# Casting weight loads, a woven first out-projection and pinned engine order in a fused attention and feed-forward kernel

## The chip, the cores and the metric

The kernel runs on one core of a Trainium2 chip. The metric is the device time of one execution in microseconds (us). Each version was run four times beside the kernel before (four to seven runs) on the same chip. All runs here lie within 1.5% of the fastest of the same kernel.

Engines: PE is TensorE's matmul, PEld its weight load, DVE is VectorE, ACT is ScalarE, POOL is GpSimd, SP is SyncE (it issues DMAs).

## The reference, cut to what matters

```python
# q, k, v: (8, 8, 576, 64) float32; w_in: (512, 2048); w_out: (2048, 512)
scores = scale * np.matmul(q, k.transpose(0, 1, 3, 2))
mask = (rel >= 0) & (rel < 64)                    # rel: query minus key position; causal window of 64
attn = softmax(np.where(mask, scores, -1e9))
x = np.matmul(attn, v).transpose(0, 2, 1, 3).reshape(4608, 512)
h = np.maximum(x @ w_in, 0.0)
out = (h * h @ w_out).astype(np.float32)
```

The 4,608 tokens are 36 chunks of 128, or 9 groups of 512. The kernel does the matmuls in 16 bits. Per chunk there is an attention (transposes of k and q, scores, values, transpose of x); per group an up-projection, a squared relu and an out-projection.

## The kernel before

Five names are used all through: T (transposes of k and q), S (scores, exp and mask), V (values, division by the row sums), X (transpose of x) and U (up-projection of one chunk, in four quarters). A scheduler that the framework runs may reorder each engine's instructions, unless the engine is pinned to the emitted order; the kernel before pins none.

```python
    def load_w_in():                       # float32 through a ring of four buffers
        def one(quar, c):
            ws = wst.tile([P, FQ], FP32, name="ws", tag="ws")
            nc.sync.dma_start(out=ws[:], in_=moe_w_in[c * P:(c + 1) * P, quar * FQ:(quar + 1) * FQ])
            nc.vector.tensor_scalar(out=w_in_sb[:, c, quar * FQ:(quar + 1) * FQ], in0=ws[:],
                                    scalar1=W_SCALE, scalar2=None, op0=ALU.mult)
        # ... 16 of them; w_out likewise, cast on GpSimd

    def transposes(i):                     # T: 8 transposes on PE, then
        # ... halo of the last chunk's keys copied on VectorE
        nc.vector.tensor_copy(out=kT[:, :, 64:192], in_=ps[:, 0])
        nc.scalar.activation(out=qT[:], in_=ps[:, 1], func=AF.Copy, scale=1.0)

    def values(i):                         # V
        for half in range(2):
            # ... 8 matmuls into av
            nc.vector.reciprocal(out=rden[:], in_=av[:, :, 64:65])
            nc.vector.tensor_tensor(out=x_sb[:, 4 * half:4 * half + 4, :], in0=av[:, :, 0:D],
                                    in1=rden[:].to_broadcast([P, 4, D]), op=ALU.mult)

    # after an up-projection's matmuls into hps: relu on ScalarE, square on VectorE
            nc.scalar.activation(out=hrelu[:], in_=hps[:], func=AF.Relu)
            nc.vector.scalar_tensor_tensor(out=..., in0=hps[:], scalar=0.0, in1=hrelu[:],
                                           op0=ALU.max, op1=ALU.mult)

    # ---- order of emission
    load(0)
    for s in load_w_in(): s()
    NFIRST = 8                             # eight chunks one by one, before any out-projection
    for i in range(1, NV - 1): load(i)
    # ... attention of chunk 0 with warm-up matmuls between
    for i in range(1, NFIRST):
        up = ffn_up_chunk(i)
        up[0](), V(i + 1), T(i + 2), up[1](), up[2](), X(i + 1), S_(i + 2), up[3]()
    for g in range(1, NTB + 1):            # steady part: three streams, evenly interleaved
        streams = [(ffn_out(g - 1), 0.0, 1.0)]
        if g >= 2 and g < NTB: streams.append((ffn_up(g), 0.0, 1.0))
        if g + 1 < NTB: streams.append((attention(g + 1), 0.0, 0.95))
        # ...
```

The softmax here doesn't subtract the row's maximum and nothing guards it: scores larger than these inputs give would overflow.

Of the kernel before, what the change touches and what calls it, by code (L numbers as in the profile page):

```python
# [13 lines left out]


def weave(*streams):

    keyed = []
    for s, (steps, lo, hi) in enumerate(streams):
        n = len(steps)  # L20
        for i, step in enumerate(steps):
            keyed.append((lo + (hi - lo) * (i + 0.5) / n, s, i, step))
    keyed.sort(key=lambda e: e[:3])
    return [e[3] for e in keyed]
# [3 lines left out]
def kernel(  # L28
# [17 lines left out]
    W_SCALE = 100.0  # L46
    OUT_SCALE = 1.0 / (W_SCALE * W_SCALE)
# [6 lines left out]
    wst = ctx.enter_context(tc.tile_pool(name="wst", bufs=4))  # L54
    stage = ctx.enter_context(tc.tile_pool(name="stage", bufs=15))
    st16 = ctx.enter_context(tc.tile_pool(name="st16", bufs=8))
    attw = ctx.enter_context(tc.tile_pool(name="attw", bufs=3))
# [8 lines left out]

    ident = const.tile([P, P], FP16, name="ident")
    make_identity(nc, ident[:])





    base = const.tile([P, 64], FP16, name="base")
    nc.gpsimd.memset(base[:], BIG)
    nc.gpsimd.affine_select(
        out=base[:], in_=base[:], compare_op=ALU.is_ge, fill=0.0, base=-1,
        pattern=[[-1, 64]], channel_multiplier=1,
    )
    nc.gpsimd.affine_select(  # L80
        out=base[:], in_=base[:], compare_op=ALU.is_ge, fill=0.0, base=64,
        pattern=[[1, 64]], channel_multiplier=-1,
    )
# [10 lines left out]
    mask_first = make_mask("mask_first", 0)  # L94
    mask_inner = make_mask("mask_inner", None)
    mask_second = make_mask("mask_second", 1)

    w_in_sb = const.tile([P, DMC, DFF], FP16, name="w_in_sb")
    w_out_sb = const.tile([P, FFC, DM], FP16, name="w_out_sb")

    NV = 8
    v_evs = [const.tile([P, H, 66], FP16, name=f"v_ev{i}") for i in range(NV)]
    v_ods = [const.tile([P, H, 66], FP16, name=f"v_od{i}") for i in range(NV)]
    for i in range(NV):
        nc.vector.memset(v_evs[i][:, :, 64:65], 1.0)
        nc.vector.memset(v_ods[i][:, :, 64:65], 1.0)
    nc.vector.memset(v_ods[0][0:64, :, 0:D], 0.0)

    def load_w_in():
        steps = []  # L110
        FQ = DFF // 4

        def one(quar, c):
            ws = wst.tile([P, FQ], FP32, name="ws", tag="ws")
            nc.sync.dma_start(out=ws[:], in_=moe_w_in[c * P:(c + 1) * P,  # L115
                                                      quar * FQ:(quar + 1) * FQ])
            nc.vector.tensor_scalar(  # L117
                out=w_in_sb[:, c, quar * FQ:(quar + 1) * FQ], in0=ws[:],
                scalar1=W_SCALE, scalar2=None, op0=ALU.mult)

        for quar in range(4):
            for c in range(DMC):
                steps.append(lambda quar=quar, c=c: one(quar, c))
        return steps

    def load_w_out():
        def one(f):
            ws = wst.tile([P, DM], FP32, name="ws2", tag="ws")
            nc.sync.dma_start(out=ws[:], in_=moe_w_out[f * P:(f + 1) * P, :])
            nc.gpsimd.tensor_copy(out=w_out_sb[:, f, :], in_=ws[:])  # L130

        return [lambda f=f: one(f) for f in range(FFC)]


    xTs = {}

    def xT_of(g):
        if g not in xTs:
            xTs[g] = xtp.tile([P, DMC, 512], FP16, name="xT", tag="xT")
        return xTs[g]  # L140

    q16s, k16s, qTs, kTs, pms, xs = {}, {}, {}, {}, {}, {}

    def load(i):

        sts = []
        for (src, nm) in ((k, "k"), (q, "q"), (v, "v")):
            st = stage.tile([P, H, D], FP32, name=f"{nm}_st", tag="st")
            b0, j0 = divmod(2 * i, NB)
            if j0 + 1 < NB:  # L150
                nc.sync.dma_start(  # L151
                    out=st[:], in_=src[b0, :, 64 * j0:64 * j0 + P, :].rearrange("h p d -> p h d"))
            else:
                nc.sync.dma_start(
                    out=st[0:64], in_=src[b0, :, 64 * j0:S, :].rearrange("h p d -> p h d"))
                nc.sync.dma_start(
                    out=st[64:P], in_=src[b0 + 1, :, 0:64, :].rearrange("h p d -> p h d"))
            sts.append(st)
        k16s[i] = st16.tile([P, H * D], FP16, name="k16", tag="k16")
        nc.gpsimd.tensor_copy(out=k16s[i][:], in_=sts[0][:].rearrange("p h d -> p (h d)"))  # L160
        q16s[i] = st16.tile([P, H * D], FP16, name="q16", tag="q16")
        nc.gpsimd.tensor_copy(out=q16s[i][:], in_=sts[1][:].rearrange("p h d -> p (h d)"))
        v_ev, v_od, v_next = v_evs[i % NV], v_ods[i % NV], v_ods[(i + 1) % NV]
        nc.gpsimd.tensor_copy(out=v_ev[:, :, 0:D], in_=sts[2][:])
        nc.gpsimd.tensor_copy(out=v_od[64:P, :, 0:D], in_=v_ev[0:64, :, 0:D])
        if i + 1 < NCK:
            nc.gpsimd.tensor_copy(out=v_next[0:64, :, 0:D], in_=v_ev[64:P, :, 0:D])

    def transposes(i):
        ps = ps_att.tile([P, 2, HP, P], FP16, name="qkT_ps", tag="ps_a")  # L170
        for s, src in enumerate((k16s, q16s)):
            for hp in range(HP):
                nc.tensor.transpose(out=ps[:, s, hp, :], in_=src[i][:, hp * P:(hp + 1) * P],  # L173
                                    identity=ident[:])
        kT = attw.tile([P, HP, 192], FP16, name="kT", tag="kT")
        if i > 0:
            nc.vector.tensor_copy(out=kT[:, :, 0:64], in_=kTs[i - 1][:, :, P:192])
        else:
            nc.vector.memset(kT[:, :, 0:64], 0.0)
        nc.vector.tensor_copy(out=kT[:, :, 64:192], in_=ps[:, 0])  # L180
        qT = attw.tile([P, HP, P], FP16, name="qT", tag="qT")
        nc.scalar.activation(out=qT[:], in_=ps[:, 1], func=AF.Copy, scale=1.0)  # L182
        kTs[i], qTs[i] = kT, qT

    def scores(i):
        sc = [ps_att.tile([P, HP, 2, 64], FP32, name=f"sc{hh}", tag="ps_a") for hh in range(2)]
        for hp in range(HP):
            for blk in range(2):
                for hh in range(2):
                    r0 = 64 * hh  # L190
                    nc.tensor.matmul(  # L191
                        sc[hh][:, hp, blk, :], kTs[i][r0:r0 + 64, hp, 64 * blk:64 * blk + P],
                        qTs[i][r0:r0 + 64, hp, 64 * blk:64 * blk + 64], start=True, stop=True)
        j0 = 2 * i % NB
        mask = mask_first if j0 == 0 else mask_second if j0 + 1 == NB else mask_inner
        pms[i] = []
        for hh in range(2):
            pm = attw.tile([P, HP, 2, 64], FP16, name=f"pm{hh}", tag=f"pm{hh}")
            nc.scalar.activation(out=pm[:], in_=sc[hh][:], func=AF.Exp,
                                 scale=1.0 / float(D) ** 0.5)  # L200
            nc.vector.tensor_tensor(out=pm[:], in0=pm[:], in1=mask, op=ALU.min)
            pms[i].append(pm)

    def values(i):
        x_sb = attw.tile([P, H, D], FP16, name="x_sb", tag="x_sb")
        for half in range(2):
            av = ps_att.tile([P, 4, 66], FP32, name="av", tag="ps_a")
            for h in range(4 * half, 4 * half + 4):
# [8 lines left out]
                out=x_sb[:, 4 * half:4 * half + 4, :], in0=av[:, :, 0:D],  # L217
                in1=rden[:].to_broadcast([P, 4, D]), op=ALU.mult)
        xs[i] = x_sb

    def to_xT(i):
        xt = ps_att.tile([P, DMC, P], FP16, name="xt_ps", tag="ps_a")
        for c in range(DMC):
            nc.tensor.transpose(out=xt[:, c, :], in_=xs[i][:, 2 * c:2 * c + 2, :],  # L224
                                identity=ident[:])
        nc.vector.tensor_copy(out=xT_of(i // 4)[:, :, (i % 4) * P:(i % 4 + 1) * P], in_=xt[:])  # L226

    def attention(g):

        steps = []  # L230
        fns = (transposes, scores, values, to_xT)
        for t in range(4 + len(fns) - 1):
            for s, fn in enumerate(fns):
                if 0 <= t - s < 4:
                    steps.append(lambda fn=fn, i=4 * g + t - s: fn(i))
        return steps

    def loads(g):
        return [lambda i=i: load(i) for i in range(4 * g, 4 * g + 4)]

# [3 lines left out]
    def ffn_up(g):  # L244
        h2s[g] = h2pool.tile([P, FFC, 512], FP16, name="h2", tag="h2")

        def one(f):
# [59 lines left out]




    load(0)
    for s in load_w_in():
        s()
# [55 lines left out]
```

## Time and profile before

| Kernel before | |
|---|---|
| time | 347.75 us median (347.43 to 350.61) |
| span of the profiled run | 345.9 us, mean granted TensorE clock 0.987 |
| first up-projection matmul, first out-projection matmul | 19.4 us, 71.4 us |
| first matmul of a full-group up-projection | 99.1 us |
| from there to the last matmul | 242.2 us |

The last three rows are starts of matmuls read from the trace. "The head" below is everything before the first matmul of a full-group (512-token) up-projection, "the steady part" what follows it.

Busy time of each engine by stretch of the kernel before (start:length, then busy us and count of instructions of each engine, granted clock, DMA share, GB/s):

```profile
40.00:50.00 10.00, 8.49 (x164) 7.49 (x162) 8.56 (x19) 5.66 (x11) 9.44 (x17) 1.00 0.99 256
50.00:60.00 10.00, 9.13 (x175) 8.14 (x173) 8.72 (x24) 6.45 (x12) 6.14 (x10) 1.00 0.76 245
60.00:70.00 10.00, 9.26 (x177) 8.22 (x175) 8.95 (x23) 5.70 (x11) 5.07 (x9) 1.00 0.82 209
...
92.00:330.00 238.00, 237.83 (x2038) 118.66 (x2036) 149.46 (x348) 122.27 (x217) 65.52 (x106) 1.00 0.40 101
```

In the chunked stage VectorE (third pair) is nearly as full as PE (first pair); from 92 to 330 us PE is idle for 0.17 us in 238.

### The profile page before, as it was taken

What the parts mean: (1) busy time and instruction counts of PE and PEld (TensorE: products, weight loads), DVE (VectorE), ACT (ScalarE), POOL (GpSimd) and SP (SyncE); (2) the same over time, 40 slices, a digit from 0 to 9 for tenths busy, and PEclk for the clock granted to TensorE, in tenths of its full rate; (3) what the DMA queues carried; (4) which work ended last, traced back from release to release, by engine and by line L of the source; (5) the groups of instructions that cost most, each with busy time, mean ns of one, the idle gap of its engine ahead of it and who ended that gap; (6) DMA issues with size and microseconds to landing.
All of it is one profiled execution on the core that took longest, in us unless ns stands there. A gap on an engine that the chain in (4) does not pass through costs nothing.

```text
span 345.9 us, 7917 instructions
## 1 busy us (share of the span) xinstructions
PE 324.3 (94%) x3146; PEld 178.2 (52%) x3146; DVE 207.9 (60%) x506; ACT 163.8 (47%) x289; POOL 121.5 (35%) x204
## 2 busy tenths in 40 slices
PE   1957888999999999999999999999999999999995
PEld 0346787875555555445545554455445544544442
DVE  2656988852666776676776657665675566544400
ACT  1123457544535646643664466436544654444411
POOL 4009895497753333316566544530000000000000
PEclk9996999999999999999999999999999999999998
DMA  7799987899972455546877757730011000000021
GB/s 200 249 252 239 234 247 252 207 230 228 243 172 61 93 121 123 121 124 155 212 185 182 170 135 184 185 87 27 23 45 36 30 32 32 30 30 32 35 88 62
DMA packets 122341, 46.65 MB, mean 135 GB/s; under 512 B 113600, under 2 KB 113600, under 8 KB 122304
## 3 DMA queue, kind: packets, MB, share of 16 engines
q1 hardware_dynamic: 122304, 46.15, 51.7%
q8 instruction: 24, 0.39, 0.5%
q14 instruction: 13, 0.11, 0.1%
HBM read 36.70 MB, written 9.44 MB: 133 GB/s over the span
## 4 chain that ended last, share of the span: by engine, by line
PE 83%; DVE 7%; DMA 5%; ACT 2%; SPq 1%; issue 1%; ACTq 0%
PE ops L296 37%; PE hps L250 28%; DMA ws<-in_moe_w_in_dram 5%; PE qkT_ps L173 4%; PE av L211 4%; PE xt_ps L224 2%; DVE h_397 L276 1%; DVE h_1087 L276 1%; DVE xT L226 1%; DVE w_in_sb L117 1%; PE hps_639 L271 1%; SPq L151 1%; SPq L115 0%; PE hps_1088 L271 0%; PE hps_1537 L271 0%
## 5 line engine op out<-in xcount | busy, mean ns | idle before, releaser
L250 PE MATMUL hps<-xT,w_in_sb 128*128 128x512 f16 x448 | 115.2, 379 | 0.0
L254 ACT ACTIVATE hrelu<-hps 128x512 f32<-128x512 f32 x112 | 66.8, 598 | 91.6 <-PE hps L250 90.9
L250 PEld LDWEIGHTS <-w_in_sb 128*128 128x128 f16 x448 | 43.7, 98 | 52.6 <-issue 0.3
L271 PEld LDWEIGHTS <-w_in_sb 128*128 128x128 f16 x512 | 31.2, 99 | 8.2 <-issue 3.9
L301 ACT ACTIVATE osb<-ops 128x512 f32<-128x512 f32 x36 | 21.6, 600 | 29.1 <-PE ops L296 28.9
L182 ACT ACTIVATE qT<-qkT_ps 128x512 f16<-128x512 f16 x36 | 21.5, 596 | 22.6 <-DVE kT L180 22.3
L216 DVE TENSOR_TENSOR x_sb<-av,rden 128x256 f16<-128x256 f32 x72 | 27.5, 415 | 0.1
L180 DVE COPY kT<-qkT_ps 128x512 f16<-128x512 f16 x36 | 15.2, 421 | 18.0 <-PE qkT_ps L173 17.8
L226 DVE COPY xT<-xt_ps 128x512 f16<-128x512 f16 x36 | 15.1, 420 | 12.7 <-PE xt_ps L224 12.7
L215 DVE RECIPROCAL rden<-av 128x4 f32<-128x4 f32 x72 | 11.4, 178 | 17.1 <-PE av L211 17.1
L255 DVE SCALAR_TENSOR_TENSOR h_5222<-hps,hrelu 128x512 f16<-128x512 f32 x16 | 11.1, 691 | 16.6 <-ACT hrelu L254 16.6
L296 PE MATMUL ops<-w_out_sb,h_1087 128*128 128x512 f16 x64 | 17.5, 380 | 0.0
L191 PEld LDWEIGHTS <-kT 64*128 64x128 f16 x576 | 11.0, 95 | 12.2 <-issue 9.6
L296 PE MATMUL ops<-w_out_sb,h_3120 128*128 128x512 f16 x64 | 16.5, 380 | 0.0
L296 PE MATMUL ops<-w_out_sb,h_2579 128*128 128x512 f16 x64 | 16.5, 380 | 0.0
L296 PE MATMUL ops<-w_out_sb,h_4199 128*128 128x512 f16 x64 | 16.5, 380 | 0.0
L296 PE MATMUL ops<-w_out_sb,h_3658 128*128 128x512 f16 x64 | 16.5, 380 | 0.0
L296 PE MATMUL ops<-w_out_sb,h_2041 128*128 128x512 f16 x64 | 16.5, 380 | 0.0
L296 PE MATMUL ops<-w_out_sb,h_4736 128*128 128x512 f16 x64 | 16.4, 379 | 0.0
L296 PE MATMUL ops<-w_out_sb,h_397 128*128 128x512 f16 x64 | 15.3, 380 | 0.0
L224 PE MATMUL xt_ps<-ident,x_sb 128*128 128x128 f16 x144 | 15.1, 222 | 0.1
L255 DVE SCALAR_TENSOR_TENSOR h_4736<-hps,hrelu 128x512 f16<-128x512 f32 x16 | 11.0, 689 | 6.8 <-ACT hrelu L254 6.4
(837 smaller groups left out, 611.1 us busy)
## 6 DMA issues: line engine op xcount, KB each, us to landing
out_dram<-osb SPq DMA_DIRECT2D x36, 256.0 KB, 2.2
k_st<-in_k_dram SPq DMA_DIRECT2D x32, 256.0 KB, 3.9
q_st<-in_q_dram SPq DMA_DIRECT2D x32, 256.0 KB, 4.0
v_st<-in_v_dram SPq DMA_DIRECT2D x32, 256.0 KB, 4.1
ws<-in_moe_w_in_dram SPq DMA_DIRECT2D x16, 256.0 KB, 4.2
k_st<-in_k_dram SPq DMA_DIRECT2D x8, 128.0 KB, 3.2
q_st<-in_q_dram SPq DMA_DIRECT2D x8, 128.0 KB, 3.0
v_st<-in_v_dram SPq DMA_DIRECT2D x8, 128.0 KB, 3.2
```

What stands on the lines that cost most here:

```text
L173: nc.tensor.transpose(out=ps[:, s, hp, :], in_=src[i][:, hp * P:(hp + 1) * P], identity=ident[:])
L180: nc.vector.tensor_copy(out=kT[:, :, 64:192], in_=ps[:, 0])
L182: nc.scalar.activation(out=qT[:], in_=ps[:, 1], func=AF.Copy, scale=1.0)
L216: nc.vector.tensor_tensor(out=x_sb[:, 4 * half:4 * half + 4, :], in0=av[:, :, 0:D], in1=rden[:].to_broadcast([P, 4, D]), op=ALU.mult)
L224: nc.tensor.transpose(out=xt[:, c, :], in_=xs[i][:, 2 * c:2 * c + 2, :], identity=ident[:])
L226: nc.vector.tensor_copy(out=xT_of(i // 4)[:, :, (i % 4) * P:(i % 4 + 1) * P], in_=xt[:])
L250: nc.tensor.matmul(hps[:], w_in_sb[:, c, f * P:(f + 1) * P], xT_of(g)[:, c, :], start=(c == 0), stop=(c == DMC - 1))
L254: nc.scalar.activation(out=hrelu[:], in_=hps[:], func=AF.Relu)
L255: nc.vector.scalar_tensor_tensor(out=h2s[g][:, f, :], in0=hps[:], scalar=0.0, in1=hrelu[:], op0=ALU.max, op1=ALU.mult)
L271: nc.tensor.matmul(hps[:, f, :], w_in_sb[:, c, (4 * fq + f) * P:(4 * fq + f + 1) * P], xT_of(g)[:, c, t0:t0 + P], start=(c == 0), stop=(c ...
L296: nc.tensor.matmul(hold["ps"][:], h2s[g][:, f, ts * P:(ts + 1) * P], w_out_sb[:, f, :], start=(f == 0), stop=(f == FFC - 1))
L301: nc.scalar.activation(out=osb[:], in_=hold["ps"][:], func=AF.Copy, scale=OUT_SCALE)
```

## The change

The intent: get both weights into 16 bits without VectorE, fill the wait for w_in with attention, give the VectorE-heavy chunk-by-chunk stage less to do, and fix the order of all engines to the emitted one. The core of the diff:

```diff
-        def one(quar, c):
-            ws = wst.tile([P, FQ], FP32, name="ws", tag="ws")
-            nc.sync.dma_start(out=ws[:], in_=moe_w_in[...])
-            nc.vector.tensor_scalar(out=w_in_sb[...], in0=ws[:], scalar1=W_SCALE, ...)
+    def load_w_in(quar):                    # casts from float32 on the way; w_out likewise
+        nc.gpsimd.dma_start(out=w_in_q[quar][:], in_=moe_w_in[...])
 ...
-        if i > 0:                           # halo copy of every chunk
-            nc.vector.tensor_copy(out=kT[:, :, 0:64], in_=kTs[i - 1][:, :, P:192])
+        if i % 4 == 0:                      # one boundary tile per group of four chunks
+            nc.vector.tensor_copy(out=kBs["b", g][:, :, 64:P], in_=kTs["k", g][:, :, 0:64])
 ...
+    def square(out, hps, hrelu):
+        nc.scalar.activation(out=hrelu, in_=hps, func=AF.Relu, scale=H_SCALE)
+        nc.vector.scalar_tensor_tensor(
+            out=out, in0=hps, scalar=0.0, in1=hrelu, op0=ALU.max, op1=ALU.mult)
 ...
+    E = mybir.EngineType
+    ctx.enter_context(tc.manual_schedule(engines={E.PE, E.Activation, E.DVE, E.Pool, E.SP}))
 ... loads of chunks 0 to 3, attention of 0 and part of 1 and 2, w_in behind the key casts of chunks 3 and 4, w_out behind that of chunk 5
+    V(1), S(2), X(1), warm(1), T(3), V(2), S(3), U(0, 0), X(2), U(1, 0), U(2, 0), V(3)
+    load_chunk(6)
+    U(0, 1), U(1, 1), X(3), U(2, 1), U(0, 2), U(1, 2), U(2, 2), U(3, 0), U(3, 1), T(4)
+    load_chunk(7)
+    U(3, 2), U(0, 3), S(4), U(1, 3), U(2, 3), U(3, 3), V(4), T(5), X(4), S(5)
 ... first out-projection, woven with attention of chunks 6 to 11 and U of 6 and 7
+    for i in range(6, 12):
+        t = 0.17 + 0.115 * (i - 6)
+        steps += [(t, T, i), (t + 0.06, S, i), (t + 0.15, V, i), (t + 0.21, X, i)]
 ... steady part, per group (positions are shares of the group)
+        steps = [((n + 0.5) / 16, out_proj, g - 1, n // 4, n % 4) for n in range(16)]
+            steps += [((f + 0.8) / 16, up, g, f) for f in range(FFC)]
+                i, t = 4 * G + j, 0.18 * j
+                    steps += [(t, T, i), (t + 0.07, S, i)]
+                steps.append((t + 0.17, V, i))
+                    steps.append((t + 0.25, X, i))
```

## The prediction

> **What bounds the kernel now.** TensorE. The table of stretches shows it busy 10.0 of every 10 us from 70 us to its last matmul at 341.8 us; only the head has slack. By the timeline the chunked up-projections (chunks 0 to 7) end at 75.4 us. I estimate: 75.4 to 341.8 us, less 1,024 matmuls of 512 columns at 0.216 us (four start 0.864 us apart), leaves 45 us for 28 chunks' attention, 1.6 us each. A chunk's up-projection, 64 matmuls, takes 3.7 us (16 in 0.92). Eight chunks at 5.3 us are 42.6 us: the head wastes 33 us.
>
> Where: first matmul at 4.4 us, a mask wait of 2.7 us, 26 warm-up matmuls in the trace; from 20 to 31 us waits for w_in (the chain has 5% w_in DMA; VectorE waits 12.1 us for it), with the granted clock at 0.5 to 0.6 from 26 to 30 us; then seven chunks at 6.4 us each. There VectorE is nearly full (8.6 to 9.0 of 10 us, 40 to 70 us). Its work per chunk, from the groups: key copies 0.33 + 0.42, masks 2 x 0.7, reciprocals 2 x 0.18, x 2 x 0.415, xT 0.42, four squarings at 0.69: 6.5 us.
>
> **What the change does.**
> 1. w_in comes as four 1 MB casting loads issued on GpSimd after chunks 0 to 3: no four-buffer ring, no 16 VectorE scalings (7.0 us). [...] No cast load is in the trace; plain w_in loads reached 352 to 379 GB/s for 2 us, about 250 in the mean. Attention of four chunks fills the time before w_in.
> 2. One pair of halo copies per group, not one copy per chunk.
> 3. The VectorE-bound head shrinks from eight chunks to six; the rest of group 1 and attention 8 to 11 run beside the first out-projection: PE has 31 us of work there, VectorE 26.
> 4. Order pinned; the steady part has the same arithmetic, so the same time at best.
>
> **Sum.** Chunks 0 to 3 land by 15 us (0.79 MB each at 250 GB/s), w_in, interleaved with chunks 4 and 5, by 32 to 36 us. After it: four quarter up-projections and chunks 4 and 5, 17 us with their chains. Head ends near 51 us (46 to 59). Then 1,024 x 0.216 + 7.4 + 30 x 1.6 = 277 us, 2 us of new waits, the 3.5 us tail, 1.8 us between span and measured time: 335 us. Without waits and with fast casts 327; slow casts give 343.
>
> **What would show it.** w_in's last quarter landing at 32 to 36 us; the first out-projection beginning near 51 us, not 71; no VectorE waits for w_in; PE about 10 of 10 from 52 us on; second out-projection to the end within 1% of before; the same tail.
>
> **What would make it wrong.** Casting loads well below 250 GB/s, or starved by chunk loads [...]: w_in at 45 us, or w_out late, and the gain halves. GpSimd issuing them late, behind casts that wait for DMA. Chunks 6 to 11 are needed every 3.8 us against 3.1 us of load: a late one stops the pinned PE. Pinned ACT and VectorE queues blocking in the steady part (1% is 2.7 us). The clock dropping around 17 to 25 us.
>
> Faster (under 340.8 us) 0.80, within 2% 0.17, slower 0.03. Prediction 335 us, 327 to 343.

## More of the kernel before

The profile page of before: busy times, two rows of the table of forty equal slices (digits are tenths busy), the chain that ended last, and three groups (name, shape, count | busy, mean ns | idle time just before, and what ended most of it).

```profile
PE 324.3 (94%) x3146; PEld 178.2 (52%) x3146; DVE 207.9 (60%) x506; ACT 163.8 (47%) x289; POOL 121.5 (35%) x204
PE   1957888999999999999999999999999999999995
DVE  2656988852666776676776657665675566544400
...
PE 83%; DVE 7%; DMA 5%; ACT 2%; SPq 1%; issue 1%; ACTq 0%
...
L182 ACT ACTIVATE qT<-qkT_ps 128x512 f16<-128x512 f16 x36 | 21.5, 596 | 22.6 <-DVE kT L180 22.3
L216 DVE TENSOR_TENSOR x_sb<-av,rden 128x256 f16<-128x256 f32 x72 | 27.5, 415 | 0.1
L215 DVE RECIPROCAL rden<-av 128x4 f32<-128x4 f32 x72 | 11.4, 178 | 17.1 <-PE av L211 17.1
```

PE is full after the head. The last line shows a healthy order on VectorE: the reciprocals wait for PE's values (17.1 us in all), that is, VectorE stands ready when they arrive.

## The result and the profile after

The changed kernel took 352.4 us median (351.49 to 352.79, four runs), against 347.75 us. Ratios here and below are the mean time of one kernel's runs over that of the other's of the same rounds, so not quite the ratio of the medians quoted; this one is 1.0111, with a 95% interval of 1.0071 to 1.015. It is 1% slower (the interval excludes 1), where 3.7% faster was predicted.

| | before | after | difference |
|---|---|---|---|
| first out-projection | 71.4 | 60.4 | -11.0 |
| first full-group up-projection (end of the head) | 99.1 | 97.1 | -2.0 |
| from there to the last matmul | 242.2 | 249.3 | +7.1 |
| span | 345.9 | 350.6 | +4.7 |

The first out-projection did start 11 us earlier, but it now carries work which before had been done ahead of it, so the milestone itself is no gain. At the end of the head 2 us were left of it, no more than single profiled runs scatter (see the table of milestones below), and the steady part gave back 7.

The profile page after, the same parts (the squarings had been split into many small groups on the page before):

```profile
PE 325.4 (93%) x3139; PEld 182.0 (52%) x3139; DVE 201.7 (58%) x475; ACT 164.8 (47%) x294; POOL 116.4 (33%) x191
PE   7749878889899999999999999999999999999995
DVE  3646756487757646764676467646764566433300
...
PE 73%; DVE 13%; ACT 5%; DMA 3%; SPq 2%; issue 2%; POOL 1%; ACTq 0%
...
L250 DVE SCALAR_TENSOR_TENSOR h<-hps,hrelu 128x512 f16<-128x512 f32 x144 | 99.2, 690 | 112.0 <-ACT hrelu L249 111.6
L168 ACT ACTIVATE qT<-qkT_ps 128x512 f16<-128x512 f16 x36 | 21.5, 597 | 61.1 <-DVE kT L167 61.1
```

PE's share of the chain fell from 83% to 73%, VectorE's rose from 7% to 13%, although VectorE has 6 us less work. ScalarE's query copies wait 61 us behind VectorE's key copies, 22 before. The stretches after:

```profile
40.00:50.00 10.00, 7.05 (x133) 6.02 (x131) 6.91 (x16) 5.90 (x11) 3.65 (x6) 0.97 1.20 191
50.00:60.00 10.00, 8.45 (x129) 7.85 (x127) 5.76 (x13) 3.90 (x8) 5.16 (x9) 0.86 1.15 217
60.00:70.00 10.00, 9.12 (x111) 5.32 (x109) 4.45 (x12) 3.94 (x8) 7.92 (x14) 1.00 1.03 208
70.00:80.00 10.00, 8.70 (x152) 6.47 (x150) 7.45 (x17) 5.21 (x11) 6.83 (x11) 1.00 0.96 208
...
92.00:330.00 238.00, 234.81 (x1974) 118.53 (x1975) 143.55 (x322) 117.92 (x212) 61.94 (x99) 1.00 0.45 99
```

No compute engine is full from 40 to 80 us: PE idles for 6.7 us in 40, and VectorE is less busy than before. The DMA engines are busy throughout (shares of 0.96 to 1.20), but of the loads PE's list of waits, of which the four longest follow, names only one of w_in, 3.4 us before the first up-projection. Even from 92 to 330 us PE idles for 3.2 us, where it had been 0.17. PE's longest waits in the changed kernel, and two of VectorE's (us in total, times, longest):

```profile
PE sc L193 <- ACT qT L168: 3.8, 10, 0.7
PE xt_ps L232 <- DVE x_sb L222: 3.6, 8, 1.0
PE hps L268 <- DMA w_in<-in_moe_w_in_dram: 3.4, 1, 3.4
PE av L217 <- DVE pm L206: 2.2, 6, 0.5
...
```

```profile
DVE h L250 <- ACT hrelu L249: 111.6, 124, 4.1
...
DVE rden L221 <- PE av L217: 0.2, 1, 0.2
```

The second fence is the symptom: VectorE waits for ScalarE's relu 124 times, and the reciprocals practically never wait for PE's values (0.2 us; 17.1 before). Nearly whenever values arrive, VectorE comes late to them. A piece of the trace of the changed kernel shows why (start us, duration, engine, line, operation, what it waited for):

```profile
45.08 0.60 ACT L249 ACTIVATE hrelu<-hps 128x512 f32<-128x512 f32 x1 [0.71 <-PE hps L268]
...
45.23 0.19 PE L217 MATMUL av<-v_ev,pm 128*64 128x65 f16 x1
...
45.71 0.69 DVE L250 SCALAR_TENSOR_TENSOR h<-hps,hrelu 128x512 f16<-128x512 f32 x1 [0.62 <-ACT hrelu L249]
46.32 0.17 DVE L221 RECIPROCAL rden<-av 128x4 f32<-128x4 f32 x1
46.53 0.42 DVE L222 TENSOR_TENSOR x_sb<-av,rden 128x256 f16<-128x256 f32 x1
...
47.01 0.28 PE L232 MATMUL xt_ps<-ident,x_sb 128*128 128x128 f16 x2 [1.03 <-DVE x_sb L222]
...
47.41 0.41 DVE L167 COPY kT<-qkT_ps 128x512 f16<-128x512 f16 x1
...
47.86 0.60 ACT L168 ACTIVATE qT<-qkT_ps 128x512 f16<-128x512 f16 x1 [2.18 <-DVE kT L167]
...
48.51 0.41 PE L193 MATMUL sc<-qT,kT 64*128 64x64 f16 x16 [0.67 <-ACT qT L168]
```

The values are there by 45.4 us. VectorE is idle, but its next instruction is a squaring, which needs a relu that ScalarE finishes only at 45.7. The squaring takes 0.69 us, then reciprocals and copies follow; PE has to wait 1.03 us for x and 0.67 us for the query copy. VectorE and ScalarE keep to the program's order in this trace: compared by line with the built program, all 475 instructions of VectorE and 293 of ScalarE's 294 (the other is a table load) start in the order in which it has them. So here a waiting instruction holds up ready ones behind it: the reciprocal at 46.32 comes 0.9 us after the last values. Whether the loss comes from it is for the experiments to say.

### The profile page after: what moved, and what is told of

Its sections match the earlier page's. It is cut to its first block, busy times and chain, and to the rows that moved or that the text cites. A ratio compares the mean times of both kernels' runs of the same rounds, so it can differ in the third digit from the quotient of the medians.

```text
span 350.6 us, 7832 instructions
## 1 busy us (share of the span) xinstructions
PE 325.4 (93%) x3139; PEld 182.0 (52%) x3139; DVE 201.7 (58%) x475; ACT 164.8 (47%) x294; POOL 116.4 (33%) x191
## 4 chain that ended last, share of the span: by engine, by line
PE 73%; DVE 13%; ACT 5%; DMA 3%; SPq 2%; issue 2%; POOL 1%; ACTq 0%
PE ops L285 31%; PE hps L256 26%; PE hps L268 6%; DVE h L250 5%; DVE pm L206 3%; ACT hrelu L249 3%; PE av L217 3%; PE qkT_ps L163 3%; PE sc L193 2%; SPq L81 2%; DVE x_sb L222 2%; DMA w_in<-in_moe_w_in_dram 2%; PE xt_ps L232 2%; DMA st<-in_v_dram 1%; ACT qT L168 1%
## 5 line engine op out<-in xcount | busy, mean ns | idle before, releaser
L250 DVE SCALAR_TENSOR_TENSOR h<-hps,hrelu 128x512 f16<-128x512 f32 x144 | 99.2, 690 | 112.0 <-ACT hrelu L249 111.6
L285 PE MATMUL ops<-w_out,h 128*128 128x512 f16 x576 | 145.6, 380 | 0.5 <-DVE h L250 0.5
L249 ACT ACTIVATE hrelu<-hps 128x512 f32<-128x512 f32 x144 | 85.9, 597 | 88.9 <-PE hps L256 69.1
L256 PE MATMUL hps<-xT,w_in 128*128 128x512 f16 x448 | 115.1, 379 | 0.0
L285 PEld LDWEIGHTS <-h 128*128 128x128 f16 x576 | 52.6, 98 | 57.2 <-issue 0.8
L256 PEld LDWEIGHTS <-w_in 128*128 128x128 f16 x448 | 42.1, 98 | 46.4
L98 POOL CAST k<-st 128x512 f16<-128x512 f32 x35 | 21.9, 626 | 89.5 <-DMA st<-in_k_dram 76.4
L268 PE MATMUL hps<-xT,w_in 128*128 128x128 f16 x512 | 36.0, 234 | 6.6 <-DMA w_in<-in_moe_w_in_dram 3.4
L202 ACT ACTIVATE pm<-sc 128x512 f16<-128x512 f32 x72 | 39.2, 600 | 5.5 <-PE sc L193 5.5
L268 PEld LDWEIGHTS <-w_in 128*128 128x128 f16 x512 | 33.3, 106 | 8.5 <-issue 4.1
L104 POOL CAST v_ev<-st 128x512 f16<-128x512 f32 x36 | 22.9, 637 | 35.9 <-DMA st<-in_v_dram 35.1
L206 DVE TENSOR_TENSOR pm<-pm,mask_inner 128x512 f16<-128x512 f16 x56 | 29.5, 551 | 6.9 <-ACT pm L202 6.3
L105 POOL COPY v_od<-v_ev 64x512 f16<-64x512 f16 x36 | 22.6, 627 | 2.3
L107 POOL COPY v_od<-v_ev 64x512 f16<-64x512 f16 x35 | 22.3, 638 | 2.0
```

Source lines behind the costliest of these rows:

```text
L98: copy(out=kq16(key, i // 4)[:, :, i % 4, :].rearrange("p a (b d) -> p a b d", d=D), in_=st[:].rearrange("p (a b) d -> p a b d", b=2))
L202: nc.scalar.activation(out=pm[:], in_=sc[hh][:], func=AF.Exp, scale=1.0 / float(D) ** 0.5)
L206: nc.vector.tensor_tensor(out=pm[:], in0=pm[:], in1=mask, op=ALU.min)
L249: nc.scalar.activation(out=hrelu, in_=hps, func=AF.Relu, scale=H_SCALE)
L250: nc.vector.scalar_tensor_tensor(out=out, in0=hps, scalar=0.0, in1=hrelu, op0=ALU.max, op1=ALU.mult)
L256: nc.tensor.matmul(hps[:], w_in_q[f // 4][:, c, f % 4 * P:(f % 4 + 1) * P], xT_of(g)[:, :, c, :], start=(c == 0), stop=(c == DMC - 1))
```

## The experiments

Theory at the start: fixing the order of the engines costs what the change gains, because attention copies stand behind work that waits. Rivals: the casting loads (with chunk loads starved beside them) cost it; or the spacing of the attention steps is too tight whoever orders them. Sixteen kernels' milestones in one table (starts of matmuls, us; each from the one profiled run):

| kernel | median us | ratio to before | first out-proj. | end of the head | from there to last matmul |
|---|---|---|---|---|---|
| before | 347.75 | 1 | 71.4 | 99.1 | 242.2 |
| the change | 352.4 | 1.0111 | 60.4 | 97.1 | 249.3 |
| e1_unpin | 341.86 | 0.982 | 58.4 | 90.9 | 244.5 |
| e1b_unpin_compute | 339.04 | 0.974 | 54.4 | 87.2 | 245.6 |
| e2_before_cast | 351.56 | 1.0102 | 39.6 | 101.1 | 244.1 |
| e2b_cast_win | 343.6 | 0.9858 | 69.9 | 94.1 | 244.1 |
| e3_spaced | 346.1 | 0.9942 | 58.8 | 95.2 | 243.4 |
| e4_pin_pe | 344.12 | 0.989 | 58.8 | 93.7 | 244.9 |
| e4_pin_actdve | 351.84 | 1.0096 | 60.1 | 95.5 | 248.5 |
| e7_free_dve | 344.03 | 0.9889 | 58.6 | 93.4 | 245.0 |
| e6_free_spaced | 337.52 | 0.9697 | 56.2 | 88.9 | 243.4 |
| e8_head | 340.54 | 0.9793 | 57.9 | 90.6 | 243.4 |
| e8_head_early | 335.49 | 0.9644 | 53.4 | 85.8 | 243.4 |
| e10_defer | 342.19 | 0.9828 | 56.3 | 92.0 | 244.8 |
| e9_pin_good | 344.91 | 0.9895 | 60.0 | 96.5 | 243.4 |
| e11_good_defer | 339.6 | 0.9747 | 54.5 | 90.2 | 243.4 |

Intervals of the ratios are at most 0.5% to either side. All were correct. A milestone of one profiled run scatters: the change and e3_spaced run the same instructions in the same order on every engine up to 96 us, and yet their heads end at 97.1 and 95.2 us. Of these 1.9 us, 1.6 arise where the change's PE ran at half clock (granted 0.5 from 49.3 to 52.7 us) and e3_spaced's did not. So differences of 2 us between heads are not read below.

### Is it the pinned order, or the loads?

**e1_unpin**: the changed kernel with nothing pinned.

```diff
-    ctx.enter_context(tc.manual_schedule(engines={E.PE, E.Activation, E.DVE, E.Pool, E.SP}))
```

> The changed kernel with no engine pinned. The scheduler then also issues the first w_in load at about 1 us and all w_in and w_out loads before chunk 3's cast. Theory 'the head is short of w_in': the first up-projection begins before 15 us instead of at 23 us, the clock stays up, and the time falls below that of the run with only the compute engines free, by 3 us or more. Rival 'casting loads starve the chunks': weights early means chunks 1 to 5 late, so the head gains nothing over that run or loses.

It took 341.86 us, 10.5 less than the change: same loads, same arithmetic. Pinning costs more than the change gains. The theory for this run, 3 us or more below the next one, failed: it is 2.8 us above it. The profile had a new PE wait of 3.6 us for transposes behind a GpSimd cast; loads and casts were reordered too.

**e1b_unpin_compute**: only POOL and SP stay pinned.

```diff
-...engines={E.PE, E.Activation, E.DVE, E.Pool, E.SP}))
+...engines={E.Pool, E.SP}))
```

> The changed kernel, with only GpSimd and SyncE pinned, so that loads come in the same order but TensorE, VectorE and ScalarE are ordered by the compiler's scheduler. Theory 'pinned compute order costs': the steady part gains about 4 us and the head's chains 1 to 4 us, so 345 to 348 us. Rival 'the head is late because of the loads, not the order': the first out-projection still begins at 59 to 61 us, and the total gains only the steady part's 4 us, about 348 us. If the pinning costs nothing: 352 us.

339.04 us, within the range that had been predicted for the change (327 to 343), and 13.4 us less than the change; it is also faster than the 345 to 348 us that the theory had given. The order of loads and of GpSimd that the change chose is good; the fixed order of the three compute engines costs 13 us, 9.9 of them in the head and 3.7 after it.

**e2_before_cast**: the kernel before with both weights loaded by casting DMAs, nothing pinned.

```diff
-            nc.sync.dma_start(out=ws[:], in_=moe_w_in[...]); nc.vector.tensor_scalar(...)
+            nc.gpsimd.dma_start(out=w_in_q[quar][:], in_=moe_w_in[...])   # and w_out alike
```

> The kernel before, with one part of the change alone: w_in and w_out as casting loads on GpSimd, nothing pinned, eight chunks in the head. Theory 'casting loads are themselves quick (about 300 GB/s of source) but starve chunk loads beside them': w_in is complete by about 18 to 20 us instead of 25, VectorE and GpSimd lose 7 and 12 us of casts, and since the head is VectorE-bound at 6.5 us per chunk, its end moves from 75 to about 68 to 71 us: 341 to 345 us in all. Rival 'casting loads are slow or starve chunks 1 to 7 so that the head waits for chunks': 347 to 352 us, with GpSimd waits for chunk loads in the head.

351.56 us. This alone would have looked like proof against casting loads, but its list of waits names the cause:

```profile
PE ops L286 <- DMA w_out<-in_moe_w_out_dram: 7.3, 1, 7.3
PE hps L261 <- DMA w_in<-in_moe_w_in_dram: 4.7, 2, 2.4
```

The free scheduler had put first out-projection matmuls ahead of attention, where PE came to them at about 32 us, before w_out was there; they started at 39.6. So the run says little of the casting of w_in, and was repeated without w_out:

**e2b_cast_win**: as e2_before_cast, w_in alone.

> The kernel before with w_in alone as casting loads; w_out stays plain loads with GpSimd casts. In the run with both, the scheduler put out-projection matmuls at 32 us, before w_out was there, and TensorE stood 7.4 us. Theory 'casting is itself worth something': without that wait the head ends 3 to 6 us earlier than before, 342 to 345 us. Rival 'casting loads starve the chunk loads and give it back': 346 to 349 us.

343.6 us, ratio 0.9858 (0.9812 to 0.9904): the casting of w_in gains 4.7 us by itself, against 348.34 us for the kernel before in the same rounds. Here everything was ordered by the scheduler, in both kernels. With e1b_unpin_compute, where the change's own loads are in place, the loads are cleared of the loss.

### Which engine's order?

**e4_pin_pe** (PE, POOL, SP pinned; ScalarE and VectorE free), **e4_pin_actdve** (the reverse: only PE freed) and **e7_free_dve** (only VectorE freed):

```diff
-...engines={E.PE, E.Activation, E.DVE, E.Pool, E.SP}))
+...engines={E.PE, E.Pool, E.SP}))                           # e4_pin_pe
+...engines={E.Activation, E.DVE, E.Pool, E.SP}))            # e4_pin_actdve
+...engines={E.PE, E.Activation, E.Pool, E.SP}))             # e7_free_dve
```

> The changed kernel with TensorE, GpSimd and SyncE pinned and VectorE and ScalarE left to the scheduler. The run with all three compute engines free took 339.0 us against 352.4 pinned. If the cost lies in VectorE's and ScalarE's fixed order (head-of-line waits before copies that TensorE needs), this run takes 339 to 342 us; if it lies in TensorE's own fixed order, 350 to 352 us.

> The mirror of the last: VectorE, ScalarE, GpSimd and SyncE pinned, TensorE free. If VectorE's and ScalarE's fixed order costs, 349 to 352 us; if TensorE's fixed order costs, 339 to 342 us. Both between (344 to 348 us) means that the two orders cost about half each.

> The changed kernel with all pinned but VectorE. With VectorE and ScalarE both free it took 344.1 us against 352.4. Theory 'it is VectorE's order (masks, key copies and squarings wait in line behind one that waits for ScalarE)': 344 to 346 us. Rival 'it is ScalarE's order': 350 to 352 us.

344.12, 351.84 and 344.03 us. Freeing PE alone gives nothing (351.84 against 352.4); freeing VectorE alone gives 8 us, and freeing ScalarE besides gives nothing more. So VectorE's fixed order is what costs, and about 5 us more come only when PE is freed with it (339.04); that is why e4_pin_pe falls between its two expectations. The trace of e7_free_dve shows what the scheduler did: counted against VectorE's other instructions, 82 of the 144 squarings come one to three places later than in the change, and none earlier.

### Which part of VectorE's order?

**e3_spaced**: everything pinned, attention steps of the steady part further apart.

```diff
-                    steps += [(t, T, i), (t + 0.07, S, i)]
-                steps.append((t + 0.17, V, i))
-                    steps.append((t + 0.25, X, i))
+                    steps += [(t, T, i), (t + 0.11, S, i)]
+                steps.append((t + 0.26, V, i))
+                    steps.append((t + 0.37, X, i))
```

> The changed kernel, with only the spacing of attention steps in the steady part widened (scores 0.11 instead of 0.07 of a group's section after the transposes, values 0.26 instead of 0.17, transposes of x 0.37 instead of 0.25). Theory 'pinned order blocks the steady part': from the second out-projection (about 92 us) to the end PE lost some 4 us in waits for the key/query copies and the masks; with the wider spacing they vanish and the time falls by 3 to 5 us to 348 to 349 us, with the first 92 us unchanged. Rival 'the loss after 92 us is of another kind [...]': no change, 352 us.

346.1 us, ratio 0.9942, a larger gain than the 3 to 5 us expected. The steady part fell from 249.3 to 243.4 us: more distance hides the late copies there. So the steady loss can be repaired by spacing too; this run doesn't tell whose lateness it is.

**e10_defer**: the changed kernel, all five engines pinned; only VectorE's squarings are emitted later, when the next scores, up-projection step or out-projection group begins. The instruction order of PE, ScalarE, GpSimd and SP was compared with the change's in the two traces and is identical; on VectorE nothing but squarings moved (72 of 144, one to six places later).

```diff
+    late = []
+    def flush():
+        while late: late.pop(0)()
     def scores(i):
+        flush()                       # likewise at the start of up and up_chunk,
+                                      # and of the first out_proj of a group
     def square(out, hps, hrelu):
         nc.scalar.activation(out=hrelu, in_=hps, func=AF.Relu, scale=H_SCALE)
-        nc.vector.scalar_tensor_tensor(...)
+        late.append(lambda: nc.vector.scalar_tensor_tensor(...))
```

> The changed kernel, everything pinned; only VectorE's squaring instructions are emitted later, behind the reciprocals, copies and key copies of the attention work that was woven between. Theory (a squaring that waits for ScalarE's relu stands in front of attention copies on the in-order VectorE, and that is most of the 8 us which freeing VectorE gave): 345 to 348, with the idle time of the squarings before ScalarE's relu falling from 112 us toward the 82 of the run with VectorE free, and ScalarE's query copies waiting less than 61 us for the key copies. Rival (another part of the order: reciprocal and copy taken in pairs, masks before key copies): 350 to 352.5, with first out-projection still at about 60 us.

342.19 us, 10 us less than the change and a little faster than with VectorE left to the scheduler (344.03); better than the theory's 345 to 348. In the profiled runs 5.1 us of the gain lie in the head, 1.6 of which may be the change's half clock at 49.3 us, and 4.5 after it. The page and VectorE's waits of this run:

```profile
PE 83%; DVE 7%; DMA 3%; ACT 3%; SPq 2%; issue 1%; POOL 1%; ACTq 0%
...
L168 ACT ACTIVATE qT<-qkT_ps 128x512 f16<-128x512 f16 x36 | 21.5, 597 | 42.9 <-DVE kT L167 42.9
```

```profile
DVE h L257 <- ACT hrelu L256: 50.5, 60, 1.7
DVE rden L228 <- PE av L224: 21.9, 29, 1.4
```

The squarings wait 50.5 us instead of 111.6, and the reciprocals again wait for PE (21.9 us; 0.2 in the change). PE's and VectorE's shares of the chain, 83% and 7%, are those of the kernel before. In the same place of the trace as above, VectorE:

```profile
42.66 1.46 DVE L257 SCALAR_TENSOR_TENSOR h<-hps,hrelu 128x512 f16<-128x512 f32 x2
44.74 0.18 DVE L228 RECIPROCAL rden<-av 128x4 f32<-128x4 f32 x1 [0.62 <-PE av L224]
44.96 0.42 DVE L229 TENSOR_TENSOR x_sb<-av,rden 128x256 f16<-128x256 f32 x1
...
45.84 0.41 DVE L167 COPY kT<-qkT_ps 128x512 f16<-128x512 f16 x1
46.31 0.42 DVE L242 COPY xT<-xt_ps 128x512 f16<-128x512 f16 x1
46.65 0.68 DVE L257 SCALAR_TENSOR_TENSOR h<-hps,hrelu 128x512 f16<-128x512 f32 x1
```

The squaring that stood in front at 45.71 now comes at 46.65, without a wait; x and the key copy come 1.57 us earlier, of which 0.6 us is that the values themselves are there earlier in this run and 0.97 the place in the order. And in the steady part PE is full again (237.84 of 238, against 234.81 in the change):

```profile
92.00:330.00 238.00, 237.84 (x1973) 118.80 (x1972) 142.98 (x314) 119.64 (x213) 62.69 (x99) 1.00 0.44 100
```

### A version that beats both

**e6_free_spaced**: e1b_unpin_compute with the spacing of e3_spaced. **e8_head**: that with PE pinned in the head alone. **e8_head_early**: that with the first quarter of w_in issued two chunks earlier (at 12.2 us instead of about 16.5), up-projections of chunks 0 and 1 ahead of chunk 3's attention, and six more warm-up matmuls (the expectation counts seven):

```diff
     cast_chunk(1)
+    load_w_in(0)
 ...
-    for quar in range(3):
+    for quar in range(1, 3):
         load_w_in(quar)
 ...
-    V(1), S(2), X(1), warm(1), T(3), V(2), S(3), U(0, 0), X(2), U(1, 0), U(2, 0), V(3)
+    V(1), warm(2), S(2), X(1), warm(3), U(0, 0), V(2), U(1, 0), X(2), T(3), U(2, 0), S(3), warm(2), V(3)
-    ..., X(3), U(2, 1), U(0, 2), U(1, 2), U(2, 2), U(3, 0), U(3, 1), T(4)
+    ..., X(3), U(2, 1), U(3, 0), U(3, 1), U(0, 2), U(1, 2), U(2, 2), T(4)
-    ..., U(2, 3), U(3, 3), V(4), T(5), X(4), S(5)
+    ..., U(2, 3), V(4), U(3, 3), T(5), X(4), S(5)
```

> Compute engines free and the attention steps of the steady part spaced wider, both at once. With free engines the trace shows only about 1.6 us of waits after 92 us. If the two remedies meet in the same waits, 337 to 339 us, 1 to 2 us below the free run; if they are independent (6.3 + 13.4 us), 333 us; if the scheduler undoes the spacing, 339 us.

> The best run so far (compute engines free, steady part spaced, 337.5 us), with TensorE pinned in the head alone. The run with TensorE pinned throughout was 5 us slower than with it free, most of it in the head by progress at 60 us. If the fixed TensorE order of the head is what costs: 341 to 343 us. If the 5 us came from the steady order: 336 to 338 us.

> As e8_head, but with the first quarter of w_in issued one chunk earlier (after chunk 1's casts, at about 12 us instead of 16.5), the first up-projections moved ahead of chunk 3's attention, one up-projection between chunk 4's values and its transposes, and 7 more warm-up matmuls. Theory 'the head waits for w_in until 23 us and then has more work than time': the first up-projection starts at 17 to 19 us, the first out-projection at 49 to 52 us instead of 56, and the time is 4 to 7 us below e8_head. Rival 'the casting load takes the bandwidth from chunks 2 and 3, and their attention comes as much later': within 2 us of e8_head.

337.52, 340.54 and 335.49 us (335.12 to 336.14; ratio 0.9644, 0.9613 to 0.9676). Pinning PE in the head cost 3 us; the earlier w_in, the changed order and the warm-ups gave 5 back, though the first out-projection came at 53.4 us and not at the 49 to 52 expected. The last is the fastest version.

Its mean granted clock was 1.0 in the profiled run against 0.979 in the change, where PE ran at half clock (granted 0.5) from 11.8 to 15.2, from 22.0 to 28.8 and from 49.3 to 52.7 us. In the 3.4 us ahead of these three stretches PE was busy for 1.85, 0.47 and 1.44 us; what lowers the clock was not tested. The clock is not where the 5 us come from: three more runs of e8_head_early had granted clocks of 0.987 to 0.988 and took 335.4 to 336.1 us, and e8_head took 340.19 us at 0.988. In the change, the one run at 0.995 took 351.49 us and the three at 0.979 to 0.981 took 352.3 to 352.8, so the clock looks worth about 1 us there, by one run. The shares of the earlier w_in, the order and the warm-ups in the 5 us were not separated.

### Does pinning as such cost?

**e9_pin_good**: the emitted order of e8_head_early, all five engines pinned. **e11_good_defer**: that with the late squarings of e10_defer.

```diff
-    pinned = tc.manual_schedule(engines={E.PE, E.Pool, E.SP})     # head only, then Pool, SP
+    ctx.enter_context(tc.manual_schedule(engines={E.PE, E.Activation, E.DVE, E.Pool, E.SP}))
```

> The emitted order of the fastest version so far (335.5 with ScalarE and VectorE scheduled freely and PE pinned in the head alone), with all five engines pinned to it. Theory (a fixed order as such costs, because the emitted order puts VectorE's copies behind squarings in any weave of this kind): 341 to 345. Rival (only the order of the changed kernel's own weave was bad): 335 to 338.

> The fastest weave with all five engines pinned (344.9 as e9_pin_good) and the same late squarings as e10_defer. Theory (the squaring in front of attention copies is the cost of any fixed order of this kind): 335 to 338.5, level with the free version of the same weave (335.5), and the idle time of the squarings before ScalarE's relu falling from 104 us to about 50. Rival (pinning costs there for another reason, such as ScalarE's or PE's place): 341 to 345.

e9_pin_good took 344.91 us, 9.4 more than the same weave with ScalarE and VectorE free (PE pinned in the head alone): squarings emitted right behind their relu harm this weave as well. The loss is all in the head (96.5 against 85.8 us), since the wide spacing already protects the steady part (243.4 in both). e11_good_defer took 339.6 us, between the two bands: the same rule gives 5.3 us back, not all 9.4. VectorE's waits, in e9_pin_good and then in e11_good_defer, turn as they did between the change and e10_defer:

```profile
DVE h L250 <- ACT hrelu L249: 102.8, 111, 4.9
...
DVE rden L221 <- PE av L217: 0.4, 1, 0.4
```

```profile
DVE h L257 <- ACT hrelu L256: 37.4, 51, 1.7
DVE rden L228 <- PE av L224: 26.0, 29, 3.9
```

What remains, about 4 us by the medians, is in the head (90.2 against 85.8). PE waits 2.6 us there for w_in, which the free version doesn't:

```profile
PE av L224 <- DVE pm L213: 2.6, 6, 0.8
PE hps L277 <- DMA w_in<-in_moe_w_in_dram: 2.6, 1, 2.6
```

The first quarter of w_in was issued at 12.4 us and landed at 20.2 (12.2 and 18.6 in the free version), and a later first up-projection follows from that (20.3 against 19.0 us). Why it landed later was not tested. The clock, 0.995 instead of 1.0, is no explanation: one run at 0.987 took 339.64 us. The remainder stays open.

## Why the prediction was wrong, point by point

**The step that failed** is item 4: "Order pinned; the steady part has the same arithmetic, so the same time at best", with "2 us of new waits" and, in the head, "17 us with their chains" from the landing of w_in to the first out-projection. These 17 us measured 26.8 (33.6 to 60.4 us), and the part from there on took 7.4 us more than the sum had (second and third row below). The prediction counted instructions and durations, and took the order as neutral. The order decides on VectorE. Putting a squaring right behind its relu makes VectorE wait 111.6 us for ScalarE, and what is ready stands behind it. Moving the squarings alone, with every engine pinned, gave 10 us back, and the 26.8 us became 22.4. With the compute engines free, the same loads and the same arithmetic ran in 339.04 us, inside the predicted range and 4 us above the prediction itself: without the order's cost the sum was near.

The prediction did name "Pinned ACT and VectorE queues blocking in the steady part (1% is 2.7 us)" as a risk, but sized it in the steady part alone, where about half of the repair lies; it gave the outcome measured, within 2% of before, a chance of 0.17. The dropping clock that it also named came (half rate from 22.0 to 28.8 us), but looks worth about 1 us by the runs above.

**The sum, term by term.** Predicted span: 51 + 277 + 2 + 3.5 = 333.5 us. Measured 350.6.

| term | predicted | measured | over |
|---|---|---|---|
| head up to the first out-projection | 51 | 60.4 | 9.4 |
| first out-projection, woven | 31 of PE's work, and 4 out-projection matmuls of the next group (0.9) | 36.7 | 4.8 |
| rest, with 2 us of waits | 247.1 (277 - 31.9 + 2) | 249.7 | 2.6 |
| tail | 3.5 | 3.9 | 0.4 |

The fourth column adds up to 17.2 us, the difference of 17.1 but for rounding. Late squarings (e10_defer) take 4.1 off the first row, 1.0 off the second and 4.5 off the third, the first two with the scatter of 2 us told above. The rest of the first row, 5.3 us (56.3 against 51), and most of the second are not explained piece by piece; the best version brought the first to 53.4.

**What held.** The last quarter of w_in landed at 33.6 us (32 to 36 predicted). VectorE's waits for w_in are gone. The casting loads were fast enough: while they were in flight they read about 280 to 330 GB/s of float32 (an estimate: the trace shows 140 to 165 GB/s written as 16-bit packets of 1,024 bytes, counted by 4 us windows, and what is read is twice that). The casting of w_in alone was worth 4.7 us in the old kernel (e2b_cast_win). An issue took GpSimd about 0.75 us (0.87 the longest), and the four loads of w_in landed 6.7 to 11.8 us after theirs. The trace shows chunk loads, issued on SyncE, and these loads moving side by side, but not in equal shares: chunk loads, which come in 256-byte packets, fell to about 40 to 50 GB/s while the 1,024-byte packets of the casting loads were in flight, from about 195 to 225 GB/s alone. Why in these shares was not tested. It didn't decide the result: GpSimd waited for these loads (76.4 us for keys alone), but PE's list of waits in the change names no chunk load, and e1b_unpin_compute ran 13.4 us faster with the same order of loads.

**What did not hold of the signs.** The first out-projection began at 60.4 us (51 predicted, 46 to 59 as range). PE was not "about 10 of 10 from 52 us on" but 8.5 to 9.1 until 80 us. The steady part was not within 1% of before but 2.9% longer (249.3 against 242.2). The tail was 3.9 us, against 3.5 in the sum and 4.2 in the kernel before, so here "the same tail" held and the sum's 3.5 was low.

**What stays open.** Freeing PE besides VectorE and ScalarE gave 5 us more (344.12 to 339.04): it reorders matmuls in the head, and which of them count was not isolated. The last 4 us of e11_good_defer against e8_head_early are in the head and mostly unexplained. The shares of the group-wise halo and the woven first out-projection in the gain were not separated.

## What to carry to other kernels

Before fixing the order of an engine that then keeps to it (as VectorE and ScalarE did in the change, 475 and 293 instructions), ask for each instruction not how long it takes but when its inputs come, and what that is ready stands behind it: in both weaves tried here an instruction that consumes another engine's fresh result did better behind copies whose inputs are there (10 and 5.3 us). In a profile this shows as a group with a large idle time before it, on an engine that is nowhere near full (VectorE was 58% busy in the change), while groups behind it (here the reciprocals) never wait for their own producers. When a change both moves work and pins the order, run it once with the compute engines unpinned: here that one run (e1b_unpin_compute) told which of the two was at fault.
